# A gated linear-attention and rational-MLP kernel on one core: the last unit's output in two PSUM slots, and a new written order of steps

## The chip, the cores and the metric

The kernel runs on one NeuronCore of a Trainium2 chip. The metric is the device time of one execution in microseconds (us), the median of several runs. The engines are PE (matrix products; PEld is its weight load), DVE (vector), ACT (scalar and activations), POOL (general purpose; here it mainly issues DMAs that cast or add) and SP (issues DMAs only). Each engine works off its own instructions in the order in which the program issued them, and waits on semaphores for the others.

## The reference

A gated linear recurrence for each of 4 batches and 8 heads (768 steps, head size 48), then a two-layer net with a rational activation on the joined heads.

```python
f = 1.0 / (1.0 + np.exp(-f_logit))
state = np.zeros((B, H, D, D)); y = np.zeros_like(q)
for t in range(S):
    state = f[:, :, t, :, None] * state + np.einsum('bhd,bhe->bhde', k[:, :, t], v[:, :, t])
    y[:, :, t] = np.einsum('bhd,bhde->bhe', q[:, :, t], state)
x = y.transpose(0, 2, 1, 3).reshape(B * S, H * D)         # 3072 x 384
h = x @ w_in                                              # 384 -> 2048
P = a[0] + a[1]*h + a[2]*h**2 + a[3]*h**3
Q = 1.0 + np.abs(b[0])*np.abs(h) + np.abs(b[1])*h**2
out = (P / (Q + 1e-6)) @ w_out                            # 2048 -> 384, float32
```

## The kernel before

The work is cut into 12 **units** of 256 tokens: unit n is batch n mod 4 and part n div 4 of the sequence, and each unit holds two chunks of 128 tokens (j = 0 and 1). For one unit:

- `ld n f/k/q/v` load the inputs. f, k and q go over SP's queue as float32, v goes over POOL's queue and is cast on the way. Each has three buffers.
- `ef`, `ls` (ACT) take the logarithm of the gate in two steps, `cs` (PE) sums it along the tokens, `A` (ACT, twice) takes exponentials of plus and minus the sum, `xa` (DVE, twice) multiplies q and k by them, `T` (PE) transposes and `Te` (DVE) copies out.
- `sc` (PE) forms the scores in two groups, `mk` (DVE) masks them, `vm` (POOL, twice) copies parts of v aside, `id` and `sv` (PE) with `ae` (ACT) and `st` (DVE) carry the state on, `yb` (PE) forms y, and `ye` (ACT) copies it out as the input of the net.
- `h n m0 m1` (PE) is the first layer for blocks m0 to m1 of 128 hidden columns (16 blocks in all). `hy` (ACT) copies it out. `sq` (DVE) or `sa` (ACT) squares it, `ab` (DVE) takes the absolute value. The denominator's logarithm comes either by `u` (PE adds the two) and `ln` (ACT), or by `zd` (a DMA on POOL's queue that adds in place) and `lz` (ACT). `ex` (ACT) turns it into the reciprocal.
- `p1`, `p2`, `pm` (DVE) form the two halves of the numerator. They are added by `ta` (a DMA on POOL's queue that adds in place) or `tv` (DVE), and `gm` (DVE) multiplies by the reciprocal.
- `o n j m0 m1` (PE) is the second layer for chunk j, `oe` copies the sums out of PSUM, and `so` (SP) stores them. The last unit is stored in four parts: `s0` on SP and `s1` on ACT's queue.
- Before the first unit `cz`, `ca`, `cb`, `cc` write constants (zeros, triangles, identity, mask), `b1_` and `ab_` load the coefficients, `fa`, `fb`, `rg` prepare them, `wi` and `wo` load the weights on POOL's queue, and `hv` is a small write that holds `wi` back until DVE has reached it.

**The order.** Nothing is scheduled by the framework (`tc.manual_schedule()`). A table in text, `ORDER`, lists some 830 steps, and the program issues them one after the other; so the table sets the order on every engine and every DMA queue. Its entries are separated by semicolons, `@s` names one of four PSUM slots. A slot is two banks, and one tile lives in it at a time: a step that takes slot s waits until whatever read the slot's last tile is done. PE's steps that take a slot are `cs`, `id` (or `sv`), `T`, `sc`, `yb`, `h`, `u` and the first `o` of a unit.

**The end before.** Both chunks of a unit's output lie in one tile of one slot, `[P, UB, 512]`. For the last unit the copy of chunk 1 (`oe 11 1 2 v`, DVE) stands in the table ahead of the last four matmuls of chunk 0 (`o 11 0 12 16`), and the copy of chunk 0 (`oe 11 0 1 s`, ACT) after them.

Where lines are named: L200 is the load of f, k, q, v; L216 and L220 the loads of w_in and w_out; L308 `ef`, L313 `ls`, L323 `cs`, L332 `A`, L348 `T`, L388 `vm`, L394 y, L474 `h`, L488 `hy`, L496 `sa`, L508 `u`, L516 `ln`, L540 `ex`, L559 `ta`, L568 `gm`, L575 `o`, L584 the stores, L590 `oe`.

Of the kernel before, what the change touches and what calls it, by code (L numbers as in the profile page):

```python
# [19 lines left out]
b1_; cz 3; cb; ld 0 f 2 4; ld 0 f 0 2; ca; cz 0; ld 0 q 2 4; cz 2; ld 0 k 2 4; cz 1; cc; ef 0 2 4  # L20
ld 0 k 0 2; fa 0; ls 0 2 4; ld 0 q 0 2; ef 0 0 2; cs 0 2 4 @0; ls 0 0 2; ld 0 v; A 0 0 2 4
id 0 0 @1; A 0 1 2 4; xa 0 0 2 4; rg; cs 0 0 2 @2; ld 1 f; xa 0 1 2 4; ae 0; A 0 1 0 2; hv 0; ab_
T 0 2 4 @0; wi 0 4; A 0 0 0 2; xa 0 1 0 2; Te 0 2 4; xa 0 0 0 2; sc 0 1 @0; ld 1 k; T 0 0 2 @2
wi 4 8; mk 0 1; vc 0; Te 0 0 2; vm 0 0 s; sv 0; vm 0 1 s; ld 1 v; sc 0 0 @2; st 0 0; ld 1 q; wi 8 16
mk 0 0; id 0 1; st 0 1; yb 0 0 4 @2; ef 1; ld 2 f; fa 1; ls 1; ye 0; cs 1 @1; fb; h 0 0 4 @2; A 1 0
A 1 1; h 0 4 8 @1; hy 0 0 4; xa 1 1; ld 2 k; id 1 0 @2; hy 0 4 8; xa 1 0; ld 2 q; ae 1; sv 1; vm 1 0
vm 1 1; ab 0 0 8; T 1 @1; ld 2 v; sq 0 0 8; Te 1; u 0 0 4 @0; ef 2; ld 3 f; u 0 4 8 @3; st 1 0
ln 0 0 4; p1 0 0 8; id 1 1; sc 1 0 @1; ln 0 4 8; st 1 1; sc 1 1 @0; mk 1 0; ls 2; ex 0 0 8; mk 1 1
id 2 0 @3; ld 3 k; cs 2 @1; pm 0 0 8; yb 1 0 4 @0; A 2 1; wo 8 12; h 0 12 16 @2; p2 0 0 8; ye 1
wo 4 8; xa 2 1; A 2 0; h 1 4 8 @0; wo 0 4; ld 3 q; tv 0 0 8; hy 0 12 16; wo 12 16; h 1 0 4 @1; ae 2  # L30
sa 1 4 8; xa 2 0; ld 4 f; hy 1 4 8; gm 0 0 8; ld 3 v; T 2 @2; hy 1 0 4; vm 2 1; h 0 8 12 @0; Te 2
vm 2 0; sa 1 0 4; sv 2; ab 1 0 8; ef 3; sc 2 0 @1; h 1 12 16 @2; st 2 0; hy 0 8 12; mk 2 0; ls 3
ld 4 k; u 1 0 4 @0; ab 0 8 16; hy 1 12 16; p1 0 8 16; cs 3 @1; ln 1 0 4; sq 0 8 16; h 1 8 12 @2
A 3 0; p2 0 8 16; u 0 12 16 @0; A 3 1; pm 0 8 16; hy 1 8 12; id 2 1; u 0 8 12 @1; ln 0 12 16; st 2 1
sc 2 1 @2; tv 0 8 16; id 3 0 @3; ld 4 q; ln 0 8 12; u 1 4 8 @0; mk 2 1; ae 3; ex 0 8 16
o 0 0 0 4 @1; o 0 0 4 8; p1 1 0 16; yb 2 0 4 @2; ln 1 4 8; o 0 1 0 4; ab 1 8 16; ye 2; xa 3 0
o 0 1 4 8; ex 1 0 8; h 2 0 4 @2; pm 1 0 8; ld 5 f; gm 0 8 16; h 2 4 8 @0; hy 2 0 4; xa 3 1; ef 4
o 0 1 8 12; sq 1 8 16; ld 5 k; o 0 1 12 16; sa 2 4 8; ld 4 v; sv 3; sa 2 0 4; p2 1 0 16; o 0 0 8 12
vm 3 0; ls 4; vm 3 1; ld 5 q; u 1 12 16 @2; st 3 0; ta 1 0 8; hy 2 4 8; pm 1 8 16; o 0 0 12 16
ln 1 12 16; id 3 1; ld 6 f; T 3 @0; st 3 1; ta 1 8 16; ef 5; ab 2 0 8; u 1 8 12 @3; Te 3; oe 0 0 2 s  # L40
zd 2 0 8; h 2 12 16 @2; ln 1 8 12; so 0 0 2; ls 5; sc 3 1 @3; sc 3 0 @0; h 2 8 12 @1; mk 3 1; ld 6 k
ex 1 8 16; ld 5 v; mk 3 0; cs 4 @3; vm 4 1; hy 2 8 12; vm 4 0; cs 5 @0; A 4 0; yb 3 0 4 @1; gm 1 0 8
A 4 1; ye 3; xa 4 0; o 1 0 0 4 @3; hy 2 12 16; o 1 1 0 4; xa 4 1; ld 6 q; h 3 4 8 @1; A 5 0
# [12 lines left out]
sq 4 8 16; lz 3 0 8; o 2 1 4 8; ab 4 8 16; T 6 @3; mk 5 1; A 7 0; o 2 1 8 12; ld 9 k; o 2 1 12 16
ex 3 0 8; p2 3 0 16; u 4 8 12 @2; xa 7 1; yb 5 0 4 @1; ta 3 0 8; ln 4 8 12; xa 7 0; ta 3 8 16
o 2 0 12 16; ye 5; p1 4 0 16; u 4 12 16 @2; vm 7 1; ld 9 q; ls 8; vm 7 0; h 5 4 8 @1; oe 2 0 2 s
ld 8 v; Te 6; ln 4 12 16; h 5 12 16 @0; pm 4 8 16; sa 5 4 8; so 2 0 2; hy 5 4 8; p2 4 0 16
sc 6 0 @2; cs 8 @3; hy 5 12 16; h 5 0 4 @1; pm 4 0 8; A 8 1; mk 6 0; h 5 8 12 @0; A 8 0; ta 4 0 8  # L60
hy 5 0 4; gm 3 0 8; sc 6 1 @2; sv 7 @3; sa 5 0 4; id 7 0; mk 6 1; ld 10 f; hy 5 8 12; o 3 0 0 4 @1
ta 4 8 16; o 3 1 0 4; gm 3 8 16; ae 7; ef 9; yb 6 0 4 @0; lz 4 0 8; st 7 0; o 3 0 4 8; p1 5 0 16
ld 10 k; o 3 0 8 12; ye 6; ab 5 0 8; o 3 0 12 16; ex 4 8 16; pm 5 0 8; zd 5 0 8; h 6 12 16 @0
xa 8 1; ld 9 v; h 6 8 12 @2; ls 9; ab 5 8 16; vm 8 1; hy 6 12 16; ld 10 q; vm 8 0; sq 5 8 16; id 7 1
o 3 1 4 8; ex 4 0 8; o 3 1 8 12; st 7 1; pm 5 8 16; u 5 8 12 @0; h 6 4 8 @3; hy 6 8 12; p2 5 0 16
ln 5 8 12; h 6 0 4 @2; gm 4 0 8; ta 5 0 8; sa 6 4 8; ab 6 8 16; T 7 @0; hy 6 4 8; ta 5 8 16
gm 4 8 16; o 3 1 12 16; sa 6 0 4; o 4 0 0 4 @3; Te 7; hy 6 0 4; o 4 1 0 4; ld 11 f; ef 10; sq 6 8 16
# [48 lines left out]
def kernel(  # L116
# [514 lines left out]
```

## Time and profile before

| what | value |
|---|---|
| median of the runs, us | 226.56 (3 runs, 225.03 to 228.58) |
| the profiled execution, us | 224.93 |
| its span, first to last instruction, us | 223.2 |
| PE busy, us | 205.2 (92%) |
| DVE busy, us | 203.3 (91%) |
| ACT busy, us | 201.1 (90%) |
| POOL busy, us | 70.4 (32%) |
| mean granted TensorE clock | 0.997 |
| bytes moved by DMA | 42.33 MB, 61984 packets |

The span is what the profiler saw between the first and the last instruction of one execution; the execution's own time is 1.7 us longer. Busy time is the time in which an engine had an instruction of its own running, issuing of DMAs left out. Matmuls overlap in the profile, so a row's duration of one matmul is longer than its step from one to the next; the chain of waits shows the steps. In the DMA tables q0 is POOL's queue, q1 the queue of SP's loads and stores.

### The profile page before, as it was taken

How to read it: one execution, taken by the hardware profiler on the slowest of the kernel's cores; microseconds unless marked ns; L12 is line 12 of the kernel's file. 1: busy time of each engine (PE TensorE's matmuls, PEld its weight loads, DVE VectorE, ACT ScalarE, POOL GpSimd, SP SyncE). 2: the span in 40 equal slices, each digit the busy share in tenths (PEclk: the TensorE clock that was granted, in tenths of full speed). 3: DMA queues.
4: the chain of work that ended last, by engine and by line, in shares of the span. 5: the costliest groups of instructions: out<-in, count | busy, mean ns of one | idle time of the engine just before them, and what ended most of it. 6: DMA issues, size and time to landing. Idle time of an engine off the chain costs nothing.

```text
span 223.2 us, 7133 instructions
## 1 busy us (share of the span) xinstructions
PE 205.2 (92%) x3128; PEld 144.0 (65%) x3128; DVE 203.3 (91%) x248; ACT 201.1 (90%) x215; POOL 70.4 (32%) x94
## 2 busy tenths in 40 slices
PE   1786799999999997999999999999999999999991
PEld 1544378566766686567777668678578587785550
DVE  6865999999789997999999999999999999999960
ACT  5645599999999999999999999999999999999960
POOL 3662930021500333107334244041395311341000
PEclk9999999999999999999999999999999999999998
DMA  6999999998999999977999999938869999597434
GB/s 156 225 230 210 237 202 204 193 248 232 170 180 244 243 184 216 260 193 144 171 233 248 209 238 244 213 74 134 171 117 184 207 188 212 112 206 150 94 91 120
DMA packets 61984, 42.33 MB, mean 190 GB/s; under 512 B 51458, under 2 KB 57346, under 8 KB 61954
## 3 DMA queue, kind: packets, MB, share of 16 engines
q0 software_dynamic: 19648, 22.61, 61.6%
q1 hardware_dynamic: 42144, 19.08, 35.0%
q8 instruction: 24, 0.39, 0.6%
q10 hardware_dynamic: 162, 0.20, 0.2%
q14 instruction: 6, 0.05, 0.1%
HBM read 25.17 MB, written 4.72 MB: 134 GB/s over the span
## 4 chain that ended last, share of the span: by engine, by line
PE 62%; ACT 20%; DMA 7%; SPq 4%; issue 3%; DVE 3%
PE op L575 26%; PE hp L474 18%; DMA fn<-in_f_logit_dram 7%; PE u L508 5%; ACT hy L488 4%; PE y L394 4%; ACT lq L516 4%; ACT qi L540 3%; PE tp L348 3%; SPq L200 3%; ACT h L496 3%; ACT A L332 3%; PE sc L369 2%; ACT lsp L313 1%; ACT fn L308 1%
## 5 line engine op out<-in xcount | busy, mean ns | idle before, releaser
L474 PE MATMUL hp<-xT,w_in_sb 128*128 128x256 bf16 x576 | 68.6, 274 | 2.3 <-issue 1.3
L575 PE MATMUL op<-w_out_sb,gall 128*128 128x384 bf16 x384 | 68.7, 326 | 1.1 <-DVE osb L590 0.6
L474 PEld LDWEIGHTS <-w_in_sb 128*128 128x128 bf16 x576 | 55.9, 98 | 12.8 <-issue 3.6
L488 ACT CAST hy<-hp 128x1024 bf16<-128x1024 f32 x48 | 49.5, 1050 | 4.1 <-PE hp L474 4.0
L575 PEld LDWEIGHTS <-gall 128*128 128x128 bf16 x384 | 36.3, 98 | 25.0 <-issue 1.8
L540 ACT ACTIVATE qi<-lq 128x2048 bf16<-128x2048 f32 (+1 forms) x25 | 46.4, 1874 | 0.0
L559 POOL DMA_DIRECT2D gall<-hy x21 | 21.3, 1109 | 64.1 <-PE hp L474 16.4
L377 DVE TENSOR_TENSOR scm<-sc,mask 128x1024 bf16<-128x1024 f32 x24 | 28.7, 1217 | 3.3 <-PE sc L369 3.3
L568 DVE TENSOR_TENSOR gall<-gall,qi 128x2048 bf16<-128x2048 bf16 (+1 forms) x25 | 29.5, 1181 | 0.7 <-ACT qi L540 0.6
L555 DVE TENSOR_TENSOR gall<-gall,h 128x2048 bf16<-128x2048 bf16 (+1 forms) x25 | 29.3, 1177 | 0.0
L388 POOL COPY vmp<-vn 128x128 bf16<-128x128 bf16 x22 | 18.1, 927 | 22.9 <-DMA vn<-in_v_dram 22.9
L525 POOL DMA_DIRECT2D z<-h x12 | 13.2, 1097 | 37.9 <-ACT xT L456 13.4
L516 ACT ACTIVATE lq<-u 128x1024 f32<-128x1024 f32 x24 | 24.5, 1048 | 0.3 <-PE u L508 0.3
L532 ACT ACTIVATE lq<-z 128x2048 f32<-128x2048 bf16 x12 | 23.5, 1956 | 0.0
L492 DVE TENSOR_TENSOR h<-hy 128x2048 bf16<-128x2048 bf16 (+1 forms) x18 | 20.9, 1166 | 0.5 <-ACT hy L488 0.5
L332 ACT ACTIVATE A<-cs 128x768 f32<-128x768 f32 (+1 forms) x26 | 18.9, 786 | 0.7 <-PE cs L323 0.5
L500 DVE TENSOR_SCALAR z<-hy 128x2048 uint16<-128x2048 uint16 (+1 forms) x25 | 16.8, 676 | 1.5 <-ACT hy L488 1.5
L550 DVE TENSOR_SCALAR hy<-hy,a_sb 128x4096 bf16<-128x4096 bf16 (+2 forms) x15 | 16.9, 1128 | 0.1
L545 DVE TENSOR_SCALAR gall<-hy,a_sb 128x4096 bf16<-128x4096 bf16 (+2 forms) x15 | 16.9, 1126 | 0.0
L323 PE MATMUL cs<-lsp,Ui 128*128 128x384 bf16 (+1 forms) x39 | 11.1, 345 | 4.8 <-ACT lsp L313 4.6
L308 ACT ACTIVATE fn<-fn 128x768 f32<-128x768 f32 (+1 forms) x13 | 10.8, 830 | 4.8 <-DMA fn<-in_f_logit_dram 4.8
L356 DVE COPY qkT<-tp 128x2048 bf16<-128x2048 bf16 (+1 forms) x13 | 14.8, 1135 | 0.4 <-PE tp L348 0.4
(69 smaller groups left out, 272.9 us busy)
## 6 DMA issues: line engine op xcount, KB each, us to landing
gall<-hy POOLq DMA_DIRECT2D x21, 512.0 KB, 7.8
z<-h POOLq DMA_DIRECT2D x12, 512.0 KB, 7.3
fn<-in_f_logit_dram SPq DMA_DIRECT2D x11, 384.0 KB, 13.2
kn<-in_k_dram SPq DMA_DIRECT2D x11, 384.0 KB, 11.9
qn<-in_q_dram SPq DMA_DIRECT2D x11, 384.0 KB, 10.6
out_dram<-osb SPq DMA_DIRECT2D x22, 192.0 KB, 4.2
vn<-in_v_dram POOLq DMA_DIRECT2D x11, 192.0 KB, 8.8
w_out_sb<-in_moe_w_out_dram POOLq DMA_DIRECT2D x4, 384.0 KB, 11.6
```

The costliest lines, as they stand in the source:

```text
L332: nc.scalar.activation(t, src, AF.Exp, scale=1.0 if x else -1.0)
L377: nc.vector.tensor_mul(t, s["sc", g].rearrange("s r a i t -> s (r a) (i t)"), mb)
L474: nc.tensor.matmul(t[:, m - m0, :].rearrange("f (j t) -> f j t", j=UB), w_in_sb[:, kk, m * P:(m + 1) * P], s["x"][:, :, kk, :], start=(kk ...
L488: nc.scalar.copy(fl(big(s, "hy", "hy", 3), m0, m1), fl(s["hp", m0], 0, m1 - m0))
L492: nc.vector.tensor_mul(fl(big(s, "h2", "h2", 2), m0, m1), fl(s["hy"], m0, m1), fl(s["hy"], m0, m1))
L516: nc.scalar.activation(fl(s["lq", g], m0 - 8 * g, m1 - 8 * g), fl(s["u", m0], 0, m1 - m0), AF.Ln, scale=rsig2, bias=1.0 + 1e-6)
L532: nc.scalar.activation(fl(s["lq", g], m0 - 8 * g, m1 - 8 * g), fl(s["z"], m0, m1), AF.Ln, scale=rsig2, bias=1.0 + 1e-6)
L540: nc.scalar.activation(fl(s["qi", g], m0 - 8 * g, m1 - 8 * g), fl(s["lq", g], m0 - 8 * g, m1 - 8 * g), AF.Exp, scale=-1.0)
L555: nc.vector.tensor_mul(fl(s["g"], m0, m1), fl(s["g"], m0, m1), fl(s["h2"], m0, m1))
L559: nc.gpsimd.dma_start(out=fl(s["g"], m0, m1), in_=fl(s["hy"], m0, m1), accum_op=ALU.add)
L568: nc.vector.tensor_mul(fl(s["g"], m0, m1), fl(s["g"], m0, m1), fl(s["qi", g], m0 - 8 * g, m1 - 8 * g))
L575: nc.tensor.matmul(s["op"][:, j, 0:DM], s["g"][:, m, C * j:C * j + C], w_out_sb[:, m, :], start=(m == 0), stop=(m == KF - 1))
```

## The change

The diff has four parts.

1. The table `ORDER` is replaced as a whole. It has the same steps as before but for the end (829 entries before, 831 after). The table of step times from which it was written had longer times for instruction blocks; that table is not part of the kernel.
2. In the last unit each chunk gets a tile and a slot of its own.
3. The last unit's two copies become four half copies `oc`: 192 of the 384 columns on ACT, the others on DVE.
4. `wm`, a step that the table does not use, gets a wider tile.

The start of the table (to unit 3's loads) and its end, before and after:

```diff
-b1_; cz 3; cb; ld 0 f 2 4; ld 0 f 0 2; ca; cz 0; ld 0 q 2 4; cz 2; ld 0 k 2 4; cz 1; cc; ef 0 2 4
-ld 0 k 0 2; fa 0; ls 0 2 4; ld 0 q 0 2; ef 0 0 2; cs 0 2 4 @0; ls 0 0 2; ld 0 v; A 0 0 2 4
-id 0 0 @1; A 0 1 2 4; xa 0 0 2 4; rg; cs 0 0 2 @2; ld 1 f; xa 0 1 2 4; ae 0; A 0 1 0 2; hv 0; ab_
-T 0 2 4 @0; wi 0 4; A 0 0 0 2; xa 0 1 0 2; Te 0 2 4; xa 0 0 0 2; sc 0 1 @0; ld 1 k; T 0 0 2 @2
-wi 4 8; mk 0 1; vc 0; Te 0 0 2; vm 0 0 s; sv 0; vm 0 1 s; ld 1 v; sc 0 0 @2; st 0 0; ld 1 q; wi 8 16
-mk 0 0; id 0 1; st 0 1; yb 0 0 4 @2; ef 1; ld 2 f; fa 1; ls 1; ye 0; cs 1 @1; fb; h 0 0 4 @2; A 1 0
-A 1 1; h 0 4 8 @1; hy 0 0 4; xa 1 1; ld 2 k; id 1 0 @2; hy 0 4 8; xa 1 0; ld 2 q; ae 1; sv 1; vm 1 0
-vm 1 1; ab 0 0 8; T 1 @1; ld 2 v; sq 0 0 8; Te 1; u 0 0 4 @0; ef 2; ld 3 f; u 0 4 8 @3; st 1 0
-ln 0 0 4; p1 0 0 8; id 1 1; sc 1 0 @1; ln 0 4 8; st 1 1; sc 1 1 @0; mk 1 0; ls 2; ex 0 0 8; mk 1 1
-id 2 0 @3; ld 3 k; cs 2 @1; pm 0 0 8; yb 1 0 4 @0; A 2 1; wo 8 12; h 0 12 16 @2; p2 0 0 8; ye 1
-wo 4 8; xa 2 1; A 2 0; h 1 4 8 @0; wo 0 4; ld 3 q; tv 0 0 8; hy 0 12 16; wo 12 16; h 1 0 4 @1; ae 2
-sa 1 4 8; xa 2 0; ld 4 f; hy 1 4 8; gm 0 0 8; ld 3 v; T 2 @2; hy 1 0 4; vm 2 1; h 0 8 12 @0; Te 2
-vm 2 0; sa 1 0 4; sv 2; ab 1 0 8; ef 3; sc 2 0 @1; h 1 12 16 @2; st 2 0; hy 0 8 12; mk 2 0; ls 3
...
-o 10 0 8 12; oe 9 0 2 s; p1 11 8 12; o 10 0 12 16; gm 11 0 8; ln 11 8 12; so 9 0 2; o 10 1 8 12
-ln 11 12 16; o 10 1 12 16; pm 11 8 12; o 11 0 0 4 @2; p2 11 8 12; ex 11 8 12; tv 11 8 12; o 11 1 0 4
-ex 11 12 16; o 11 0 4 8; gm 11 8 12; o 11 1 4 8; oe 10 0 2 s; gm 11 12 16; o 11 1 8 12; so 10 0 2
-o 11 1 12 16; o 11 0 8 12; oe 11 1 2 v; o 11 0 12 16; s1 11 1 2; s0 11 1 2; oe 11 0 1 s; s1 11 0 1
-s0 11 0 1
+b1_; cz 1; ca; ld 0 f 2 4; ld 0 f 0 2; cz 2; ld 0 q 2 4; cz 0; cb; cz 3; ld 0 k 2 4; cc; ef 0 2 4
+ld 0 k 0 2; fa 0; ls 0 2 4; ld 0 q 0 2; ef 0 0 2; cs 0 2 4 @0; ls 0 0 2; ld 0 v; A 0 0 2 4
+id 0 0 @1; rg; xa 0 0 2 4; cs 0 0 2 @2; ab_; ae 0; A 0 1 2 4; hv 0; A 0 1 0 2; wi 0 4; xa 0 1 2 4
+ld 1 f; A 0 0 0 2; xa 0 1 0 2; T 0 2 4 @0; xa 0 0 0 2; Te 0 2 4; T 0 0 2 @2; ld 1 k; wi 4 8; ld 1 q
+sc 0 1 @0; Te 0 0 2; vc 0; mk 0 1; sc 0 0 @2; vm 0 0 s; sv 0; vm 0 1 s; mk 0 0; ld 1 v; wi 8 16
+st 0 0; fa 1; yb 0 0 4 @2; fb; id 0 1; ye 0; ld 2 f; st 0 1; ef 1; h 0 0 4 @2; ls 1; id 1 0 @1
+hy 0 0 4; cs 1 @0; ae 1; h 0 4 8 @2; A 1 1; ld 2 k; A 1 0; xa 1 1; hy 0 4 8; xa 1 0; ld 2 q; sv 1
+ld 2 v; ab 0 0 8; T 1 @2; vm 1 0; sq 0 0 8; vm 1 1; st 1 0; u 0 0 4 @0; Te 1; ef 2; ld 3 f; id 1 1
+u 0 4 8 @3; ln 0 0 4; st 1 1; sc 1 1 @2; p1 0 0 8; ln 0 4 8; sc 1 0 @1; mk 1 0; ls 2; mk 1 1
+ex 0 0 8; id 2 0 @1; ld 3 k; cs 2 @3; pm 0 0 8; yb 1 0 4 @2; A 2 0; wo 12 16; h 0 12 16 @0; p2 0 0 8
+A 2 1; wo 4 8; tv 0 0 8; ae 2; ye 1; wo 0 4; h 0 8 12 @3; ld 3 q; hy 0 12 16; wo 8 12; xa 2 0
+h 1 0 4 @2; hy 0 8 12; gm 0 0 8; ld 4 f; vm 2 1; ef 3; h 1 4 8 @0; xa 2 1; ld 3 v; sa 1 0 4
+ab 0 8 16; vm 2 0; h 1 8 12 @3; ls 3; p1 0 8 16; hy 1 0 4; sq 0 8 16; sv 2; hy 1 8 12; T 2 @2
+st 2 0; p2 0 8 16; sa 1 4 8; id 2 1; u 0 12 16 @3; ld 4 k; st 2 1; hy 1 4 8; Te 2; u 0 8 12 @1
+ln 0 12 16; cs 3 @0; ab 1 0 8; ln 0 8 12; sc 2 1 @3; pm 0 8 16; u 1 0 4 @2; A 3 0; mk 2 1
+u 1 4 8 @1; A 3 1; ln 1 0 4; sc 2 0 @0; xa 3 1; h 1 12 16 @3; ex 0 8 16; ld 4 q; mk 2 0
+o 0 0 0 4 @2; tv 0 8 16; yb 2 0 4 @0; hy 1 12 16; o 0 1 0 4; xa 3 0; ye 2; id 3 0 @3; p1 1 0 16
...
+oe 9 0 2 s; u 11 8 12 @3; ex 11 0 8; so 9 0 2; p2 11 12 16; o 10 1 8 12; pm 11 8 12; o 10 0 8 12
+pm 11 12 16; ln 11 8 12; gm 11 0 8; o 10 0 12 16; o 10 1 12 16; ln 11 12 16; tv 11 12 16
+o 11 0 0 4 @3; ex 11 8 12; tv 11 8 12; o 11 1 0 4 @2; ex 11 12 16; o 11 0 4 8; gm 11 8 12
+o 11 1 4 8; oe 10 0 2 s; gm 11 12 16; o 11 0 8 12; so 10 0 2; o 11 0 12 16; o 11 1 8 12; oc 11 0 0 s
+oc 11 0 1 v; o 11 1 12 16; s1 11 0 1; s0 11 0 1; oc 11 1 0 s; oc 11 1 1 v; s1 11 1 2; s0 11 1 2
```

The code:

```diff
     def o(n, j, m0, m1, sl=None):
         s = unit(n)
-        if sl is not None:
-            s["op"] = slot(sl, [P, UB, 512], F32, "op")
+        if sl is not None and n == B * NCC - 1:
+            s["op", j] = slot(sl, [P, 512], F32, "op")
+        elif sl is not None:
+            t = slot(sl, [P, UB, 512], F32, "op")
+            s["op"] = t
+            for i in range(UB):
+                s["op", i] = t[:, i]
         for m in range(m0, m1):
-            nc.tensor.matmul(s["op"][:, j, 0:DM], s["g"][:, m, C * j:C * j + C], w_out_sb[:, m, :],
+            nc.tensor.matmul(s["op", j][:, 0:DM], s["g"][:, m, C * j:C * j + C], w_out_sb[:, m, :],
                              start=(m == 0), stop=(m == KF - 1))
...
+    def oc(n, j, c, eng):
+        s = unit(n)
+        if "osb" not in s:
+            s["osb"] = ms.tile([P, UB, DM], F32, name="osb")
+        cc = slice(c * DM // 2, (c + 1) * DM // 2)
+        (nc.scalar.copy if eng == "s" else nc.vector.tensor_copy)(s["osb"][:, j, cc], s["op", j][:, cc])
```

Among the moves on the queues: SP issues `ab_` ahead of `ld 1 f`, and several stores stand ahead of one more load than before (`so 2` ahead of `ld 9 q`, for one). POOL issues `ld 2 v` ahead of the two `vm` of unit 1, and `ld 3 v` between the two of unit 2. ACT comes to `ef 3` after `hy 0 8 12`, with `sa` and `hy` of unit 1 behind it.

## The prediction

> **What bounds the kernel now.** I read the page first, then the windows by stage, the chain of waits with its opening, the DMA traffic of single windows, and the end of the timeline. Times are microseconds (us) from the span's start.
>
> ```profile
> PE 205.2 (92%) x3128; PEld 144.0 (65%) x3128; DVE 203.3 (91%) x248; ACT 201.1 (90%) x215; POOL 70.4 (32%) x94
> ...
> 0.00:25.00 25.00, 16.14 (x267) 10.95 (x268) 17.55 (x54) 12.64 (x22) 13.25 (x29) 1.00 1.04 206
> ...
> 25.00:215.00 190.00, 185.66 (x2843) 131.30 (x2842) 184.49 (x193) 187.16 (x193) 57.20 (x66) 1.00 0.99 192
> ```
>
> In the second and third lines the columns after the length are the busy time of PE, PEld, DVE, ACT and POOL, then the granted clock, the DMA share and GB/s. From 25 to 215 three engines are busy at once, 185 to 187 of 190. The change keeps all this work, so a new order can win there only what is idle: 2.8 on ACT, 4.3 on PE, 5.5 on DVE. The first 25 are another matter: ACT is busy for 12.6 and waits largely for DMA.
>
> ```profile
> 9.59 15.19 DMA fn<-in_f_logit_dram
> 24.78 0.02 issue
> 24.80 0.84 ACT fn L308
> ...
> 34.04 1.82 ACT hy L488 x2
> 35.86 0.93 ACT h L496
> 36.79 0.73 ACT fn L308
> ```
>
> Here is the chain (start, length, what). It hangs on unit 2's f, which lands at 24.8 and is used at once; from there ACT is the chain, but for gaps of half a us, to 62.3, then PE nearly to the end. The last line is `ef 3`; the ACT timeline starts it at 36.65. Its f was issued at 20.45 and took 15.6 to land: 36.0, so it came 0.6 before it was needed. That margin is what I watch.
>
> **The parts of the change.**
>
> *Start.* The memsets and the constants change places; all are done by 3.6 in the timeline before and no user starts earlier than that on them, so I cost them at nothing (their whole DVE sum is below 2). `rg` and `ae 0` now stand ahead of one A: `ae` is 0.18, so one xa comes some 0.3 later. Both transposes now stand ahead of both masks. Followed through with the durations of the timeline (two T of 1.0, two Te of 0.69, two masks of 1.22), the second mask ends at 12.4 where it ended at 13.0: 0.5 earlier for y. Nothing comes of it, because `ef 2` still waits for f at 24.8, with the same ACT steps ahead of it in both orders. `ab_`, two small DMAs of 1.10 and 0.79 on SP, now goes ahead of `ld 1 f`: that f lands near 12.5 and not 10.6. Its user `ef 1` now stands behind `ye 0`, near 14; that wait covers it, and without the cover it would cost 1.9. The hold is lifted 0.4 earlier, so w_in starts 0.4 earlier. I take the sum as 0, between -0.5 and +1 for f of unit 2.
>
> *Unit 3's f against `ef 3`: the main term.* Two things change. ACT now comes to `ef 3` sooner: before it ran four more steps first (two `sa`, two `hy`) and lacked one `hy`. At the chain's 0.93 and 0.91 that is 2.8 net, so it arrives at about 34.0. And POOL's `ld 2 v` moves ahead of the two vmp copies of unit 1, which had waited for v until 21.71: it was issued at 23.35, now right after the last w_in, near 17.9. The traffic of four windows (18 to 21, 21 to 25, 25 to 28, 30 to 36) shows what that does:
>
> ```profile
> q0 software_dynamic: 944, 0.23, 76.4%
> q1 hardware_dynamic: 924, 0.35, 67.2%
> ...
> q0 software_dynamic: 401, 0.70, 92.6%
> q1 hardware_dynamic: 403, 0.15, 20.7%
> ...
> q0 software_dynamic: 828, 0.21, 68.8%
> q1 hardware_dynamic: 1459, 0.55, 68.1%
> ...
> q0 software_dynamic: 1077, 0.80, 85.2%
> q1 hardware_dynamic: 1077, 0.41, 38.8%
> ```
>
> Columns are packets, MB and share. Where both queues have work they move one packet each, so q1 (f, k, q) gets little whenever q0's packets are large: 0.15 MB in 4 beside w_in, 0.41 in 6 beside w_out, 0.35 in 3 beside v. Only in the third window q0 ran nearly empty for a while, because v had not been issued, and q1 moved 0.55 MB in 3. From the end of w_in (25.3) to the landing of f at 36.0, q1 moved 0.50 (25.3 to 28.3), 0.08 (28.3 to 30) and 0.41: 0.99 MB. After the change v follows w_in directly: 0.35 by 28.3, then w_out's rate of 0.068 a us for the other 0.64, 9.4 us: f lands at 37.7. Ends: 36.0 if nothing shifts, since the bytes ahead of it are the same; 39.8 if q1 has only w_out's rate from 25.3 on (0.99 over 0.068). I take 37.7, as v's rate is measured on a like DMA.
>
> So ACT waits from 34.0 to 37.7. Behind it stand `sa 1 0 4` and `hy 1 0 4`, whose slot T of unit 2 waits for; PE has two more h to do and then nothing. What is late next: from `ef 3` to the second A of unit 3 ACT has eleven steps, 9.3 in all (`ef` 0.73, `ls` 0.73, two `sa` and two `ln` 0.93, three `hy` 0.91, two A 0.70). The second scores of unit 2 take that A's slot; scores, mask and two handovers are another 1.8. So y of unit 2 starts at 37.7 + 11.1 = 48.8; before, 46.58. PE's work listed ahead of it (h 1.31, o 0.65, u 0.86, y 1.11 and so on, pitches of the chain) was 31.7 and is 30.8. PE is late by 2.2 + 0.9 = **3.1**. At 36.0 it would be 1.4, at 39.8 5.2.
>
> *The middle.* Before, PE needed 172.5 from that y to its last matmul for 164.2 of listed work: 8.3 lost. I keep 8.3. Both ends: two gaps of 1.14 and 1.10 at 84 and 87, in which PE waited for nothing that the profile shows, may go (-2.2), or others come. The DMA additions get shorter leads. Counted in DVE work between the last product and the `gm` that uses the sum, the shortest were 5.8, 6.1 and 7.3 and are 4.9, 5.9, 5.9, 6.3 and 7.4. They land in 4.5 to 8.7 (median 7.8). The shortest before made DVE wait for nothing, since theirs landed in 4.5 and 4.7; the four shortest at the median and 0.3 for the issue would cost 3.2 + 2.2 + 2.2 + 1.8 = 9.4 at most, and cover by other waits makes it less. I take 0, with -2.2 and +4 for the range. SP's stores now stand ahead of a few more loads (`so 2` ahead of `ld 9 q`); counted in listed work those have 15 us and more to their users against median landings of 10.6 to 13.2: nothing, unless a store held SP for some 3 longer. `wm` is changed, but no step of the order calls it: nothing.
>
> *The end.*
>
> ```profile
> 217.67 0.56 DVE L590 COPY osb<-op 128x384 f32<-128x384 f32 x1 [1.81 <-PE op L575]
> ...
> 218.28 0.81 PE L575 MATMUL op<-w_out_sb,gall 128*128 128x384 bf16 x4 [0.65 <-DVE osb L590]
> ...
> 219.13 0.48 ACT L590 COPY osb<-op 128x384 f32<-128x384 f32 x1 [3.31 <-PE op L575]
> ```
>
> The last four matmuls of one chunk wait 0.61 for the copy of the other: one slot, so they take turns. With a slot each this goes: -0.6. Half copies (192 columns) are not in the trace. ACT: below 0.48 (384 columns), above 0.21 (8 elements); I take 0.30 by the step from 384 to 768 (0.48 to 0.85). DVE: between 0.15 and 0.56, taken 0.33. Side by side the pair would be 0.1 shorter than the copy of 0.48. But both halves lie in one slot, and the row above shows that two engines on one slot take turns: 0.30 + 0.33 + 0.06 = 0.69, +0.2. The first pair and its ACT store issue (0.54) lie beside four matmuls. The end gives **-0.4**, between -0.8 and 0 (the second slot waits for one more `ln`).
>
> "PSUM — Partial Sum Buffer" of the Trainium skill, section "PSUM bank collisions raise a hardware error", speaks against side-by-side copies: two engines must not touch one bank and quadrant at once, reads against reads included. By it the halves can only take turns and the split itself loses; no row here shows two engines reading one bank.
>
> *Sum.* 0 + 3.1 + 0 - 0.4 = +2.7. The profiled execution took 224.93 (span 223.2 and 1.7 around it), so 227.6. The median shown, 226.56, is 0.72% above it; moved by that, **229.3**, 1.2% slower. By the ends of f alone: 36.0 gives +1.0 and 227.6, 39.8 gives +4.8 and 231.4. A measurement of this kernel can tell about 2% from no change: 222.0 and 231.1.
>
> **Rivals.** *A: f lands late enough to pass 2%* (slower). One place, ACT's `ef 3`: it decides from a landing of 39.5 on and gives 231.4 at 39.8, more if unit 2's f is late too. For it: w_out is issued sooner behind v, at about 23.4 for 24.27. Against: q1's bytes are the same, and w_in ends 0.4 sooner. 0.28.
>
> *B: the additions come late* (slower). `gm` waits at the short leads; from 2.0 of such waits the time is 224.93 + 4.7 = 229.6, moved 231.3. For it: the shorter leads; against: late in the kernel they landed in 4.5 to 7. 0.13.
>
> *C: not slower.* f of unit 3 lands by 34.0, `ef 3` waits for nothing, the lag of 3.1 is -0.6, and with the end -1.0: 223.9, moved 225.5. If both gaps of PE go too, 221.7, moved 223.3. Against: f landed at 36.0 with less beside it. Over 2% faster needs still 1.3 more from the idle time. 0.16, of it 0.06 beyond 2%.
>
> *D: the change does not do what it says*: the last matmuls wait for the slot's `ln` as long as for the copy. That is +0.6 on any case, and is within the forecast's 0.43.
>
> **How the numbers follow.** Forecast 0.43 (slower, within 2%, own range 226.5 to 231), A 0.28, B 0.13, C 0.16. Slower by over 2%: 0.28 + 0.13 = 0.41. Faster by over 2%: 0.06. Within: 0.43 + 0.10 = 0.53. The range leaves out the best of C below 223.3 and A and B together beyond 234.5 (both at their prices: 224.93 + 4.8 + 2.0 = 231.7, moved 233.4, and 1 for f of unit 2).
>
> **What would show it.** In the profile after: `ef 3` with an idle time of 2 to 6 put down to its DMA, f landing at 37 to 40; v of unit 2 issued near 18; y of unit 2 at 48 to 50; no wait of PE at the last matmuls; two half copies one after the other. Wrong if `ef 3` waits for nothing, if ACT's chain to 62 is as unbroken as before, or if `ef 2` starts far from 24.8.

## The result, and the profile after

| | before | after |
|---|---|---|
| median of 4 runs, us | 226.63 (225.03 to 228.58) | 234.09 (231.98 to 235.01) |
| ratio, 95% interval | 1 | 1.034 [1.0239, 1.0442] |
| profiled execution, its span | 224.93, 223.2 | 233.97, 232.2 |
| mean granted clock of TensorE | 0.997 | 0.970 |
| `ef 2`, `ef 3` start | 24.80, 36.65 | 26.50, 41.63 |
| y of unit 2 starts | 46.58 | 56.02 |
| from there to the end of the span | 176.6 | 176.2 |

The ratios here and below leave out executions over 1.5% above the fastest of their kernel; the medians are of all. The changed kernel is 3.4% slower. The forecast said 1.2% and 226.5 to 231 for its own case; the measured 234.09 lies beyond that, in the place of rival A, and inside the whole range of 223.3 to 234.5 by only 0.4. The last two rows of the table are the case in short: all of it is lost before y of unit 2, and what follows is half a us shorter. `ef 3` before, and y of unit 2 before and after:

```profile
36.65 0.87 ACT L308 ACTIVATE fn<-fn 128x768 f32<-128x768 f32 x1
...
46.58 0.35 PE L394 MATMUL y<-qkT,state 128*32 128x128 bf16 x12
...
56.02 0.35 PE L394 MATMUL y<-qkT,state 128*32 128x128 bf16 x12
```

Then the busy times on the profile page of the kernel after:

```profile
PE 209.5 (90%) x3117; PEld 145.9 (63%) x3128; DVE 205.4 (88%) x249; ACT 201.8 (87%) x216; POOL 72.4 (31%) x94
```

Its windows (start and end, length, busy time of PE, PEld, DVE, ACT and POOL, granted clock, DMA share, GB/s):

```profile
0.00:25.00 25.00, 15.25 (x263) 10.62 (x265) 17.66 (x53) 12.25 (x21) 14.22 (x31) 0.97 1.02 201
25.00:63.00 38.00, 31.05 (x433) 20.56 (x432) 28.02 (x29) 28.48 (x32) 4.21 (x8) 0.84 1.04 191
63.00:200.00 137.00, 135.54 (x2250) 97.62 (x2256) 134.62 (x136) 136.03 (x142) 49.07 (x51) 1.00 0.96 185
```

The same windows of the kernel before, where the prediction showed only the sum of the later two:

```profile
25.00:63.00 38.00, 36.00 (x594) 24.95 (x600) 35.74 (x38) 38.00 (x44) 10.60 (x16) 1.00 1.16 210
63.00:200.00 137.00, 134.66 (x2185) 97.72 (x2168) 134.30 (x135) 134.16 (x138) 44.60 (x49) 1.00 0.99 193
```

From 25 to 63 ACT was busy without a break before and now lacks 9.5 us; the span is longer by 9.0. Beyond 63 all three engines are as full as they were. PE's busy time has grown by 4.3 although its work is the same; the clock of 0.84 in that window goes with it, and I come back to it.

The chain of waits of the kernel after (start, length, what), at the place where the prediction showed it before:

```profile
22.75 18.85 DMA fn<-in_f_logit_dram
41.63 0.84 ACT fn L308
42.47 0.91 ACT h L496
43.39 0.73 ACT lsp L313
44.12 0.91 ACT hy L488
45.07 1.86 PE tp L348 x16
46.94 0.32 PE sv L424
47.26 0.43 PE u L508
```

It hangs no longer on unit 2's f, as before, but on unit 3's: issued at 22.75, landed 18.85 later. `ef 3` uses it at once; behind it come `sa 1 0 4`, `ls 3` and `hy 1 0 4`, and only then PE has a free slot for T of unit 2. The same place in the timeline, with the idle time ahead of each instruction in brackets:

```profile
17.92 0.92 POOL L200 DMA_DIRECT2D vn<-in_v_dram  x1
...
26.50 0.84 ACT L308 ACTIVATE fn<-fn 128x768 f32<-128x768 f32 x1 [5.21 <-DMA fn<-in_f_logit_dram]
...
41.63 0.84 ACT L308 ACTIVATE fn<-fn 128x768 f32<-128x768 f32 x1 [4.53 <-DMA fn<-in_f_logit_dram]
...
45.07 1.86 PE L348 MATMUL tp<-ident,qkp 128*128 128x128 bf16 x16 [4.72 <-ACT hy L488]
```

v of unit 2 is issued at 17.92 where it was 23.35. ACT comes to `ef 3` at 37.1 and waits 4.53; PE stands for 4.72. The traffic in the four windows the prediction used (18 to 21, 21 to 25, 25 to 28, 30 to 36), now after the change (packets, MB, share):

```profile
q0 software_dynamic: 890, 0.27, 79.2%
q1 hardware_dynamic: 854, 0.32, 61.6%
...
q0 software_dynamic: 419, 0.67, 90.2%
q1 hardware_dynamic: 424, 0.16, 22.0%
...
q1 hardware_dynamic: 982, 0.37, 70.8%
q0 software_dynamic: 944, 0.19, 70.7%
...
q0 software_dynamic: 1090, 0.81, 86.3%
q1 hardware_dynamic: 1086, 0.41, 38.9%
```

The one window that differs is the third: q1, the queue of f, k and q, moved 0.37 MB beside v, where it had 0.55 because q0 was almost empty at first (30 packets from 25.5 to 26.5). In the others the two queues again move one packet each, and q1 with its small packets gets 0.04 to 0.11 MB a us. The page "DMA: Bandwidth & Descriptors" of the Trainium skill, section "Queues, rings and completion order", states the rule behind it: each DMA engine goes round the queues that have work, a packet from each. The equal counts (419 and 424, 1090 and 1086) agree with taking turns; whether the page's packet is what the profile counts as one, no row here shows.

The end of the kernel after:

```profile
226.56 0.32 ACT L604 COPY osb<-op 128x192 f32<-128x192 f32 x1 [1.51 <-PE op L581]
226.91 0.36 DVE L604 COPY osb<-op 128x192 f32<-128x192 f32 x1 [1.82 <-ACT osb L604]
...
227.89 0.32 ACT L604 COPY osb<-op 128x192 f32<-128x192 f32 x1 [1.01 <-PE op L581]
228.24 0.36 DVE L604 COPY osb<-op 128x192 f32<-128x192 f32 x1 [0.97 <-ACT osb L604]
```

Each DVE half waits for the ACT half. From the last matmul's end, where ACT's half starts, to the end of the pair is 0.71 us, where the single copy took 0.48. No matmul waits for a copy any more.

### The profile page after: what moved, and what is told of

Same layout as the page of the kernel before. It is cut to its first block, busy times and chain, and to the rows that moved or that the text cites. A ratio compares the mean times of both kernels' runs of the same rounds, so it can differ in the third digit from the quotient of the medians.

```text
span 232.2 us, 7108 instructions
## 1 busy us (share of the span) xinstructions
PE 209.5 (90%) x3117; PEld 145.9 (63%) x3128; DVE 205.4 (88%) x249; ACT 201.8 (87%) x216; POOL 72.4 (31%) x94
## 3 DMA queue, kind: packets, MB, share of 16 engines
HBM read 25.17 MB, written 4.72 MB: 129 GB/s over the span
## 4 chain that ended last, share of the span: by engine, by line
PE 41%; DVE 20%; DMA 11%; ACT 10%; SPq 9%; issue 5%; ACTq 0%; DVEq 0%
PE op L581 16%; PE hp L474 11%; SPq L200 8%; DMA fn<-in_f_logit_dram 8%; PE u L508 5%; DMA gall<-hy 3%; DVE gall L568 3%; DVE h L492 3%; PE tp L348 3%; PE y L394 3%; ACT hy L488 2%; DVE gall L545 2%; ACT qi L540 2%; DVE gall L555 2%; DVE scm L377 2%
## 5 line engine op out<-in xcount | busy, mean ns | idle before, releaser
L581 PEld LDWEIGHTS <-gall 128*128 128x128 bf16 x384 | 36.1, 98 | 24.4 <-DVE gall L568 2.2
L488 ACT CAST hy<-hp 128x1024 bf16<-128x1024 f32 x48 | 48.7, 1035 | 3.0 <-PE hp L474 2.8
L388 POOL COPY vmp<-vn 128x128 bf16<-128x128 bf16 x22 | 20.4, 993 | 28.5 <-DMA vn<-in_v_dram 22.9
L516 ACT ACTIVATE lq<-u 128x1024 f32<-128x1024 f32 x24 | 24.4, 1044 | 1.9 <-PE u L508 1.9
L525 POOL DMA_DIRECT2D z<-h x12 | 14.3, 1189 | 26.9 <-DVE z L500 12.1
L308 ACT ACTIVATE fn<-fn 128x768 f32<-128x768 f32 (+1 forms) x13 | 10.5, 811 | 11.1 <-DMA fn<-in_f_logit_dram 11.1
L348 PE MATMUL tp<-ident,qkp 128*128 128x128 bf16 x192 | 14.8, 234 | 5.4 <-ACT hy L488 4.7
L332 ACT ACTIVATE A<-cs 128x768 f32<-128x768 f32 (+1 forms) x26 | 18.9, 788 | 0.3 <-PE cs L323 0.3
L500 DVE TENSOR_SCALAR z<-hy 128x2048 uint16<-128x2048 uint16 (+1 forms) x25 | 17.3, 693 | 1.0 <-ACT hy L488 0.9
L348 PEld LDWEIGHTS <-qkp 128*128 128x128 bf16 x192 | 12.8, 104 | 7.7 <-issue 5.4
## 6 DMA issues: line engine op xcount, KB each, us to landing
vn<-in_v_dram POOLq DMA_DIRECT2D x11, 192.0 KB, 11.1
```

Source lines behind the costliest of these rows:

```text
L348: nc.tensor.transpose(t[:, x, i, p, :], s["qk"][:, x, i, 2 * p:2 * p + 2, :].rearrange("t h d -> t (h d)"), ident)
L488: nc.scalar.copy(fl(big(s, "hy", "hy", 3), m0, m1), fl(s["hp", m0], 0, m1 - m0))
L516: nc.scalar.activation(fl(s["lq", g], m0 - 8 * g, m1 - 8 * g), fl(s["u", m0], 0, m1 - m0), AF.Ln, scale=rsig2, bias=1.0 + 1e-6)
L581: nc.tensor.matmul(s["op", j][:, 0:DM], s["g"][:, m, C * j:C * j + C], w_out_sb[:, m, :], start=(m == 0), stop=(m == KF - 1))
```

## Experiments

The theory after the result: `ld 2 v`, moved ahead of two copies on POOL, makes f of unit 3 late, and `ef 3`, which now stands ahead of the step that frees T's slot, turns that into a stop of PE. The rivals: the new start alone does it (its other moves, `ab_` among them); the later order does it (additions, stores, the end); PE's half clock does it.

**Which part of the table.** At several places both tables have issued the same set of steps; two of them are behind `yb 1`, and behind `hy 2 12 16` (about 62 us). They can be cut there and put together anew, with slots renamed to fit. In the labels A is a part of the new table and B of the old: start, second part, rest with the end.

```diff
-ORDER = before: start | second part | rest and end
+seg_ABB: start of after  | second part of before | rest and end of before
+seg_BAB: start of before | second part of after  | rest and end of before
+seg_BBA: start of before | second part of before | rest and end of after
+seg_AAB: start of after  | second part of after  | rest and end of before
```

> The table is cut in three where both orders have issued the same set of steps: start (to y of unit 1), second (to hy 2 12 16, about 62 us), rest with the end. Here only the start is the new one. Theory 1 (late loads, then a slowed PE): the new start alone makes f of unit 2 land near 26.5 and f of unit 3 near 41; before's second part comes to ef 3 near 38, waits some 3, and the time is 2.0 to 3.0% above before. Theory 2 (the loss lies in the rest of the table, in sums in place that come late): within 1% of before.

> Only the second part is the new one (ef 3 earlier in ACT's order). Theory 1: f of unit 3 lands at 36 as before, ACT comes to ef 3 at 34 and waits 2; 0.3 to 1.0% above before. Theory 2: within 0.5%.

> Only the rest with the end is the new one, with a slot for each of the last two chunks and half copies. Theory 1: between 0.5% below and 0.3% above before; the wait at the last matmuls is gone. Theory 2: 2.5 to 3.5% above, with DVE waiting for the sums in place.

> Start and second part are the new ones, the rest and the end are before's. Theory 1: as slow as the changed kernel or a little more, 3 to 4% above before, ef 3 waits 4 to 5 for f landing near 41 and PE runs for some us at half clock afterwards. Theory 2: within 1%. If the parts add up, it is the sum of the two single ones; if more, the late load and the early ef 3 make each other worse.

| | median, us | ratio to before, 95% | `ef 3` starts, idle before it | y of unit 2 |
|---|---|---|---|---|
| ABB | 229.24 | 1.0138 [1.0075, 1.0201] | 41.99, 2.69 | 53.17 |
| BAB | 227.04 | 1.0017 [0.9964, 1.0069] | 35.34, 0 | 47.18 |
| BBA | 225.09 | 0.9955 [0.9911, 0.9998] | 37.64, 0 | 47.57 |
| AAB | 233.80 | 1.0341 [1.0255, 1.0427] | 42.39, 3.37 | 55.63 |

(ABB's profiled execution lies 2.4 us above its median; its rows are read for what waits, not for sizes.) The rest of the table, with the new end, gains a little behind the old parts and nothing that shows behind the new ones (AAB has 3.41%, after 3.40%); all of the loss is in the first 62 us. ABB's 1.4% lies between its two expectations. BAB's 0.2% is what Theory 2 expected: f of unit 3 landed at 31.4 there and `ef 3` did not wait. The parts don't add up: 1.38 + 0.17 = 1.55%, and AAB, which has both, is at 3.41%. The new start and the new second part make each other worse by some 1.9%, with intervals of 0.5 to 0.9% on each figure. The start brings the late f; the old second part lets T of unit 2 go ahead of `ef 3` (T starts at 37.24 in ABB), the new one puts it behind (45.83 in AAB, 45.07 after).

**One step each.** `ld 2 v` moved back, `ab_` moved back, and both:

```diff
-a_v2:  sv 1; ld 2 v; ab 0 0 8; T 1; vm 1 0; sq 0 0 8; vm 1 1; st 1 0
+a_v2:  sv 1; ab 0 0 8; T 1; vm 1 0; sq 0 0 8; vm 1 1; ld 2 v; st 1 0
-a_ab:  cs 0 0 2; ab_; ae 0; A 0 1 2 4; hv 0; A 0 1 0 2; wi 0 4; xa 0 1 2 4; ld 1 f; A 0 0 0 2
+a_ab:  cs 0 0 2; ae 0; A 0 1 2 4; hv 0; A 0 1 0 2; wi 0 4; xa 0 1 2 4; ld 1 f; ab_; A 0 0 0 2
```

> The changed kernel with one step moved back: POOL issues ld 2 v behind the two vmp copies of unit 1. Theory 1a (v's small packets beside q1 are the cause): f of unit 3 lands at 38 to 39.5 instead of 41.6, ef 3 waits 2 to 3, PE cools less; 1.0 to 2.0% above before. Theory 1b (the queue is already behind since the start, by ab_ and w_in): no change, 3 to 3.5% above.

> The changed kernel with ab_ moved back behind ld 1 f on SP. Theory 1a: f of unit 2 lands 0 to 1 earlier than 26.5, f of unit 3 within 1 of 41.6; 2.5 to 3.4% above before. Theory 1b: f of unit 2 lands near 24.8 and f of unit 3 near 39.5, 1 to 2% above.

> Both moves back (ld 2 v, ab_). If these two are all that is wrong in the start, f of unit 2 lands at 24.8, f of unit 3 at 36 to 37, ef 3 waits 2 to 3 and the time is 0 to 1% above before, like the new second part with the old start. If something else in the start holds the loads (w_in 0.3 earlier, the order of PE), it stays at 2% or more.

a_v2 came to 227.17 us, 1.0067 [1.0025, 1.0109]; a_ab to 233.31, 1.0365 [1.0269, 1.0461]; a_v2_ab to 227.57, 1.0038 [0.9977, 1.0099]. One step of 831, moved on POOL past two copies, carries most of the loss; the place of `ab_` carries nothing that can be measured in the time. a_v2 did better than either expectation, which had `ef 3` still waiting; and in a_v2_ab f of unit 2 landed at 27.2, not at the 24.8 that these two moves would have explained. The timeline of a_v2 at the same step:

```profile
36.42 0.85 ACT L308 ACTIVATE fn<-fn 128x768 f32<-128x768 f32 x1
```

No idle time is shown: f of unit 3 landed at 36.0. From 25 to 28, q1 of a_v2 moved 0.67 MB where the kernel after moved 0.37.

**The step alone, in the kernel before.** Only `ld 2 v` is moved forward, nothing else:

```diff
-b_v2 (before): ae 1; sv 1; vm 1 0; vm 1 1; ab 0 0 8; T 1; ld 2 v; sq 0 0 8
+b_v2 (before): ae 1; sv 1; ld 2 v; vm 1 0; vm 1 1; ab 0 0 8; T 1; sq 0 0 8
```

> The kernel before with one step moved forward: POOL issues ld 2 v ahead of the two vmp copies of unit 1. If this step alone is the cause in the start, it does what the whole new start did with the old rest: f of unit 3 lands at 40 to 42, ef 3 waits 2 to 4, 1.0 to 1.8% above before. If it needs something else of the new start, within 0.6%.

228.51 us, 1.0171 [1.0085, 1.0257]. Two lines of its ACT timeline, `ef 2` and `ef 3`:

```profile
24.91 0.84 ACT L308 ACTIVATE fn<-fn 128x768 f32<-128x768 f32 x1 [3.11 <-DMA fn<-in_f_logit_dram]
39.46 0.84 ACT L308 ACTIVATE fn<-fn 128x768 f32<-128x768 f32 x1 [2.56 <-DMA fn<-in_f_logit_dram]
```

Unit 2's f is where it was (24.8), unit 3's lands at 39.4 instead of 36.0, y of unit 2 starts 2.8 later and the span is 2.8 longer (1.2% in the profile, 1.7% in the runs). That is the prediction's mechanism with nothing else in it.

**The place of `ef 3`.** In the kernel after, `ef 3` and its `ls` are moved behind three `hy` and two `sa`:

```diff
-a_ef3:  vm 2 1; ef 3; h 1 4 8 ... h 1 8 12; ls 3; p1 0 8 16 ... hy 1 4 8; Te 2
+a_ef3:  vm 2 1; h 1 4 8 ... h 1 8 12; p1 0 8 16 ... hy 1 4 8; ef 3; ls 3; Te 2
```

> The changed kernel with ef 3 and ls 3 moved behind hy 1 4 8 on ACT; all loads as changed. Theory 1 (ACT's place of the wait turns a late load into a stop of PE): ACT does its two sa and three hy while f is still out, comes to ef 3 near 39, waits 2 to 3; PE goes on with T of unit 2 and stays at full clock; 1.0 to 2.2% above before. If the late load alone sets the time, no change: 3% or more.

229.59 us, 1.0191 [1.0098, 1.0283]: about half of the loss goes. f lands as late as after (41.2), but ACT comes to `ef 3` only at 43.08 and waits for nothing. I had expected a wait near 39; ACT was later than that because it waited for PE in the steps before. PE no longer stops for long, the clock is 1.00 from 34 on, and y of unit 2 starts at 50.51.

**The half clock.** In the kernel after, the matmuls from 45 to 51 run at half the clock. Three windows of two us of the kernel after, the first with PE standing, the others with the clock of 0.50:

```profile
42.00:44.00 2.00, 0.00 (x0) 0.00 (x0) 0.97 (x2) 2.00 (x3) 0.00 (x0) 1.00 1.45 193
...
46.00:48.00 2.00, 1.78 (x12) 1.27 (x12) 0.71 (x2) 1.76 (x2) 0.00 (x0) 0.50 1.00 247
48.00:50.00 2.00, 2.00 (x5) 0.64 (x5) 2.00 (x3) 1.00 (x1) 0.00 (x0) 0.50 0.92 239
```

To price it, a_warm has PE compute one block four times over (same result) while it would stand still:

```diff
-        for m in range(m0, m1):
+        for m in list(range(m0, m1)) * (4 if (n, m0) == (1, 8) else 1):
```

> The changed kernel in which h 1 8 12, the last work PE has before it stops, is computed four times over into the same place, to the same result, so that PE is busy until about 44. Theory 1 (half clock after the stop is a cost of its own): f of unit 3 lands and ef 3 waits as in the changed kernel, but PE keeps the clock of 1.00 from 44 to 52, the transposes of unit 2 take 1.1 instead of 1.9, and 1 to 3 us of the 7.7 come back: 2.0 to 3.0% above before. Theory 3 (ACT is behind anyhow, PE's clock there costs nothing): 3.2 to 3.7%.

239.37 us, 1.0614 [1.0507, 1.0722]: slower still, against both expectations. Two of its windows of two us:

```profile
46.00:48.00 2.00, 2.00 (x55) 1.66 (x54) 1.04 (x2) 1.44 (x2) 0.00 (x0) 1.00 0.91 226
48.00:50.00 2.00, 2.00 (x12) 0.94 (x10) 2.00 (x4) 2.00 (x3) 0.00 (x0) 1.00 0.86 225
```

And a row of its PE timeline, with the idle time ahead of it:

```profile
123.83 0.23 PE L394 MATMUL y<-scm,vn 64*32 64x128 bf16 x2 [2.80 <-issue]
```

The clock stayed at 1.00 as meant. T of unit 2 starts 1.8 later than after (46.83: the extra matmuls were in its way), y of unit 2 0.9 earlier (55.12). T to y took 8.29; it took 10.95 in the kernel after, and 8.40 in a_v2, in BAB and in a_v2_ab, all at full clock. So the half clock costs 2.55 to 2.66 there. The rest of a_warm is worse for another reason: from y to the end it needs 181.0 against 176.2. Most of that is two stops of PE, 1.03 at 104 and 2.80 at 121 (the row above), in the middle of a run of y matmuls, waiting for nothing that the profile shows. What they are I did not settle; the total of this run is therefore no price of the clock.

**A version that is a little faster than both.** BBA, with the load of the last half of w_in split in two:

```diff
-bba_wi (BBA): ld 1 q; wi 8 16; mk 0 0
+bba_wi (BBA): ld 1 q; wi 8 12; wi 12 16; mk 0 0
```

> Old start and second part with the new rest and end (the fastest so far), and the last load of w_in issued as two halves of 4 blocks (packets of 1024 bytes for 2048). By the packets taking turns, q1 gets about 0.06 MB a us instead of 0.04 while w_in flows, f of unit 2 lands 0.5 to 1.5 earlier than 24.8 to 25.8, and the time is 0.5 to 1.2% below before. If the halves only take longer, f of unit 2 stays and so does the time: 0.2 to 0.6% below.

224.07 us, 0.9931 [0.9897, 0.9966]: 0.7% faster than the kernel before, but not distinguishable from BBA's 0.9955 [0.9911, 0.9998]. The direction of the traffic is as expected: from 18 to 25.3, q1 moved 0.65 MB (0.55 to 0.58 in before, BAB, BBA and bba_whole) and q0 0.83 (BBA 0.95). The landings show nothing of it: f of unit 3 landed at 32.5, in BBA at 37.0, and in bba_whole below, without the split, at 30.9. As `ef 3` doesn't wait in any of them, little of this can reach the end.

**Whole copies at the end**, in BBA: chunk 0 on DVE, chunk 1 on ACT, slots still apart.

```diff
-bba_whole (BBA): oc 11 0 0 s; oc 11 0 1 v ... oc 11 1 0 s; oc 11 1 1 v
+bba_whole (BBA): oc 11 0 2 v ... oc 11 1 2 s
-        cc = slice(c * DM // 2, (c + 1) * DM // 2)
+        cc = slice(0, DM) if c == 2 else slice(c * DM // 2, (c + 1) * DM // 2)
```

> Old start and second part with the new rest, each of the last two chunks in its own slot, but copied whole: chunk 0 by DVE, chunk 1 by ACT. If half copies take turns, the last copy takes 0.48 after the last matmul where the pair takes 0.7, so the end is 0.2 shorter (0.1%): by the end of the timeline, the times can't tell it. If they lay side by side, 0.1 longer.

224.91 us, 0.9984 [0.9939, 1.0029], not distinguishable from BBA. The row of its last copy in the timeline:

```profile
217.47 0.48 ACT L604 COPY osb<-op 128x384 f32<-128x384 f32 x1 [2.89 <-PE op L581]
```

And the last pair in the timeline of BBA:

```profile
219.08 0.32 ACT L604 COPY osb<-op 128x192 f32<-128x192 f32 x1 [1.01 <-PE op L581]
219.43 0.36 DVE L604 COPY osb<-op 128x192 f32<-128x192 f32 x1 [0.97 <-ACT osb L604]
```

0.48 against 0.71: the split costs 0.23 in the profile, 0.1% of the time, which the medians can't show.

**All profiles beside each other.** What lands when, sorted by where `ld 2 v` stands:

| | v of unit 2 issued | f of unit 2 lands | f of unit 3 issued | it lands | took | y of unit 2 | y to end |
|---|---|---|---|---|---|---|---|
| before | 23.35 | 24.8 | 20.45 | 36.0 | 15.6 | 46.58 | 176.6 |
| BAB | 23.93 | 22.5 | 19.39 | 31.4 | 12.0 | 47.18 | 177.5 |
| BBA | 23.75 | 25.8 | 21.85 | 37.0 | 15.2 | 47.57 | 175.8 |
| bba_wi | 23.75 | 24.4 | 20.12 | 32.5 | 12.4 | 46.34 | 175.4 |
| bba_whole | 23.56 | 21.7 | 18.84 | 30.9 | 12.1 | 46.09 | 175.5 |
| a_v2 | 23.14 | 26.2 | 22.95 | 36.0 | 13.1 | 48.27 | 176.3 |
| a_v2_ab | 22.44 | 27.2 | 22.33 | 37.5 | 15.2 | 49.65 | 176.3 |
| b_v2 | 17.79 | 24.8 | 21.03 | 39.4 | 18.4 | 49.36 | 176.6 |
| ABB | 18.35 | 27.3 | 23.70 | 42.0 | 18.3 | 53.17 | 176.8 |
| AAB | 17.52 | 27.7 | 23.70 | 42.4 | 18.7 | 55.63 | 177.0 |
| a_ab | 17.14 | 25.6 | 21.89 | 40.3 | 18.4 | 53.56 | 177.0 |
| a_ef3 | 17.84 | 27.1 | 23.39 | 41.2 | 17.8 | 50.51 | 176.3 |
| a_warm | 17.41 | 27.9 | 23.74 | 42.5 | 18.8 | 55.12 | 181.0 |
| after | 17.92 | 26.5 | 22.75 | 41.6 | 18.9 | 56.02 | 176.2 |

With v issued near 18 the f of unit 3 takes 17.8 to 18.9 (7 profiles), with v issued near 23 it takes 12.0 to 15.6 (7 profiles), whatever else differs. Each kernel has one profile here, and single landings scatter: BBA and bba_whole issue the same steps but for the last copies, and f of unit 3 lands at 37.0 in one and at 30.9 in the other. Save for a_warm, the stretch from y of unit 2 to the end is 175.4 to 177.5 in every kernel, so the start of y of unit 2 tells the time of the whole.

## Why the prediction was right and where it was too small

The sum gave +2.7 us on the profiled execution; it was +9.0. That the range held is in part luck: its upper bound was set for A and B together with f of unit 2 one us late, B did not happen, and the half clock, which no bound held, took its place. Of the signs named, the wait of `ef 3` (4.53), v's issue near 18, the end without a wait and the half copies one after the other came; f landed later than 37 to 40 and y of unit 2 later than 48 to 50. By its own steps:

- **The start, costed at 0 (-0.5 to +1 for f of unit 2): wrong.** f of unit 2 landed 1.7 later, beyond the bound. It is the new start itself: f of unit 2 lands at 21.7 to 25.8 behind the old start (6 profiles) and at 25.6 to 27.9 behind the new one (8), also with `ld 2 v` and `ab_` back (27.2). I had followed PE's, DVE's and ACT's steps there and taken f's landing as fixed. Which of the other moves does it stays open; no run tells them apart. It is likely part of the 0.67% that a_v2 keeps (f of unit 2 1.4 late, y of unit 2 1.7 late), but a_v2 also lost 1.1 to a half clock, shown in the last section; how the two share the 0.67% is not shown.
- **`ld 2 v` and the rates beside it: right.** Issue near 17.9, as predicted; q1 beside v 0.37 MB in 3 us (0.35 taken), beside w_out 0.41 in 6 (0.41 taken). One reading was wrong: q0 was nearly empty in the third window not "because v had not been issued". It had, at 23.35; it was the packets that came later, 6 on q0 from 25.5 to 26 and 154 from 26.5 to 27.
- **f of unit 3 at 37.7: mis-sized, by 3.9.** In b_v2, v's move alone makes it 39.4, so 3.4 later than before and not 1.7; the other 2.2 come with the new table, which issues this f at 22.75 where b_v2 does at 21.03. (One profile each: the split is rough.) The step that failed is the 0.99 MB that q1 had to move from 25.3 on, carried over from the trace of before. After the change it moved 0.40 to 28.3, 0.12 to 30, 0.41 to 36 and 0.44 to 41.6, 1.37 in all. Of the 0.38 more, 0.14 is arrears, what q1 was behind by at 25.3 (q1 moved 2.07 + 0.52 from 5 to 25.3; before, 2.18 + 0.55). b_v2 has the same 2.07 + 0.52 and moved 1.23 from there to its landing, so v's move alone brings 0.24 of the 0.38. Beyond the arrears, no row explains what is left.
- **ACT at `ef 3` at 34.0: late by 3.1** (37.1), for `ef 2`'s 1.7 and PE's half clock from 24 to 26 and 30 to 34. It made no difference, since f came later still.
- **From `ef 3` to y of unit 2, 11.1: it took 14.39.** 2.55 to 2.66 of the 3.3 is the half clock, which the prediction never priced: it said that PE has "two more h to do and then nothing", and did not ask what a PE that stands for 4.7 us does next. The page "TensorE: Matmul & The Clock Gate" of the Trainium skill, section "HAM oscillation — how this bites in real kernels", has the rule against it, no idle gaps of PE above some 3.4 us. This stop agrees: 4.72, then a clock of 0.50 from 46 to 50.
- So y of unit 2 came 7.2 later than the 48.8 predicted: 3.9 + 2.6 + 0.7 unaccounted.
- **Middle and end: right, with a small gain.** From y to the end 177.1 was predicted (227.6 less 1.7 and 48.8) and 176.2 measured. BBA shows it alone, 175.8 and -0.45%. The end's half copies took turns, 0.71 (0.69 predicted), and the matmuls' wait of 0.61 is gone. Two readings behind the bounds were off: of the two gaps only the one at 84 is PE's (at 87.37 the chain goes over DVE, and PE runs h from 87.21 on), and the additions before landed in 4.5 to 10.7, not 4.5 to 8.7.
- **The rivals.** A is what happened: its place, its mechanism, and its condition (f at 39.5 or later, unit 2's f late too). I gave it 0.28, holding against it that "q1's bytes are the same"; they were not. Carried on to a landing of 41.6 the sum gives +6.6, and with 2.6 for the half clock +9.2; measured +9.0. B is out: in the kernel after one `gm` waited 0.6 for a sum in place. C is out, `ef 3` waited. D is out, no matmul waited at the end. The forecast's side was right for its stated reason; b_v2, which holds that reason alone, is 1.7% slower, near the 1.2% forecast. The other 1.7% comes only where the new second part meets the late f: ABB, with the new start and the old second part, is 1.4% slower, no more than b_v2, and there PE stops behind `ef 3` for 2.14, after the change for 4.72.

## What to carry to other kernels

A load that is issued earlier can take its packets from the loads already on the way, as one v issued 5.4 sooner did here: count the bytes and the arrears of the other queue up to the landing that something waits for, and expect them to grow with the shift, before calling an earlier issue harmless. Where a step may wait for a DMA, look at what stands behind it on its engine: the same late f cost 1.9% with `ef 3` behind three `hy` and two `sa` and 3.4% with it ahead of them. When a wait leaves TensorE idle for several us, price the matmuls behind it at half clock as well.

## What was unexpected in the hardware

The half clock does not need one long gap. In the kernel after it followed a stop of 4.72. But a_v2 had it from 29 to 33 with no gap of PE longer than 1.33 us between 22 and 36. Its windows of two us there; from 26 to 30 PE was busy for 0.94 and 0.68 of 2 each:

```profile
26.00:28.00 2.00, 0.94 (x34) 0.57 (x33) 2.00 (x3) 1.81 (x3) 1.36 (x2) 1.00 1.47 262
28.00:30.00 2.00, 0.68 (x10) 0.34 (x10) 2.00 (x3) 2.00 (x3) 0.00 (x0) 0.83 1.46 199
30.00:32.00 2.00, 2.00 (x47) 0.86 (x47) 1.97 (x3) 2.00 (x2) 1.60 (x3) 0.50 1.25 204
```

A rule by the longest gap alone would have missed it. A low busy share does not tell it either. From 26 to 29.4, first in BBA, whose clock stayed at 1.00, then in BAB, whose clock was 0.50 from 30 to 32:

```profile
26.00:29.40 3.40, 1.20 (x39) 0.70 (x37) 3.24 (x5) 3.40 (x5) 2.98 (x4) 1.00 1.51 231
...
26.00:29.40 3.40, 2.33 (x58) 1.41 (x57) 3.40 (x5) 3.40 (x4) 2.19 (x3) 1.00 1.38 273
```

PE was busy for 1.20 of 3.4 in the kernel that kept its clock and for 2.33 in the one that lost it. What decides is open. In a_v2 the half clock was not free: the chain of waits runs over PE there.

```profile
29.64 0.37 PE sv L428 x8
30.02 1.30 PE cs L323 x4
31.32 1.42 PE y L394 x60
32.74 2.75 PE hp L474 x24
```

From this `sv` to the first h (32.67 in the timeline) a_v2 took 3.03; the kernel before took 1.94 for the same steps at full clock (28.26 to 30.20), so some 1.1 went there.
